# Keys and queries of four tiles loaded first, and one written order of four engines up to the first feed-forward matmul

## The chip, the cores and the metric

The kernel runs on one core of a Trainium2 chip. The metric is the device time of one execution in microseconds, here the median of three runs. A core has TensorE (PE, matmuls; its weight loads are shown apart as PEld), VectorE (DVE), ScalarE (ACT), GpSimd (POOL) and a queue engine, SyncE (SP), which here issues nearly all loads. Each of them works through its own list of instructions in order.

## The reference

Attention by chunks, then two feed-forward layers. q, k, v have 4 x 8 heads, 768 positions and 64 dimensions. Each chunk of 32 queries sees 8 memory keys and the keys from 16 before to 8 after it:

```python
for c in range(nc):
    k_full = np.concatenate([mem_k, k_ctx], axis=2)
    v_full = np.concatenate([mem_v, v_ctx], axis=2)
    scores = scale * np.matmul(q_c, k_full.transpose(0, 1, 3, 2))
    scores = scores - np.max(scores, axis=-1, keepdims=True)
    a = np.exp(scores)
    a = a / (np.sum(a, axis=-1, keepdims=True) + 1e-09)
    out[:, :, c_start:c_end] = np.matmul(a, v_full)
```

With the result laid out as x of 3072 tokens by 512, layer 1 is `h = x @ w_in; g = h - tanh(h); x = g @ w_out`, with a hidden width of 2048, and layer 2 the same with `g = max(h, 0) + alpha * min(h, 0)`.

## The kernel before

The tokens are 24 tiles of 128. A block is four tiles (512 tokens), so layer 1 has six blocks of 16 f-steps, one for each 128 of the hidden width. An f-step is a product h of 12 matmuls (`emit_h`, L274), the function g (`emit_g`, L289 to L299) and a product y of 12 (`emit_y`, L313). Every operand is kept as a high and a low half, and three of the four products of halves are made (`PASS`). The first matmul of h needs only the high halves; the second needs the low half of x, the third the low half of the weight.

Before the first h of block 0 the four tiles of its tokens go through attention. For a tile t: `emit_scores` makes the scores on PE (L590) into two PSUM banks, takes the maximum on DVE (L610, or L614 from tile 3 on), subtracts it (on POOL at L611 for tiles 0 to 2, with a copy of the scores by ACT at L609; on DVE at L615 after that) and takes the exponent on ACT (L619). `emit_soft` sums on DVE (L625 to L627), multiplies by the reciprocal on POOL (L628), and turns the result: for tiles 0 to 3 by matmuls with an identity on PE (`emit_turn`, L654 and L661, two halves hh) and a copy by ACT into the one buffer `ebuf` (L666); later by a DVE transpose and eight small copies (L635 to L644). `emit_pv` multiplies by the values (L674) and writes the token tile into the ring as high half by ACT (L681) and low half by DVE (L682).

Layer 1's weights arrive as raw 64-bit words. `split_w` makes two halves of each of an f-step's two weight tiles: a scaled copy by ACT (L105), three bit operations on DVE (L108, L111, L115; `to_f32`), then the high half by ACT (L121) and the low half by POOL (L122). `more_w` does that for one f-step and starts the loads of the step `AHEAD` later. In the opening loop it is called after tiles 1, 4 and 5 (`EARLY_W`), and in block 0 once for each f-step.

PSUM has eight banks: four in `ps_y` (turned tiles, early weight words, later y), two in `ps_h` (value products, h) and two in `ps_a` (scores, later weight words). Instructions are put in order by a planner that works with simulated times and the order of the code; within `tc.manual_schedule` the named engines keep the written order, and `tc.issue_after(i)` puts what is issued in it behind i on i's engine. Before, only SP's first loads are written by hand. While block 0 runs, a plan says after which half f-step the operations of tiles 4 and later come.

Of the kernel before, what the change touches and what calls it, by code (L numbers as in the profile page):

```python
# [7 lines left out]
FP32 = mybir.dt.float32  # L8
# [11 lines left out]
PERIOD = 20  # L20
LP, SLACK, LAST_C = 3, 2, 5
SPACE = 6
FIRST = 1
EARLY_W = (1, 4, 5)
PE_T = 4
ANCHOR = 'exp'
SUB_POOL = 3
ACT_COPIES = 4
BLOCKS1 = [4] * 6
# [2 lines left out]
AHEAD = 5  # L32
# [5 lines left out]
def chunk_attention_two_ffn_kernel(  # L38
# [51 lines left out]
    def load_raw(l, i, name):  # L90
        f, side = divmod(i, 2)
        src_i, src_o = (w_in1, w_out1) if l == 0 else (w_in2, w_out2)
        if l == 1 and f % 2:
            raw = ac.tile([128, 512], U64, tag="pk", name=name)
        else:
            raw = w_p.tile([128, 512], U64, tag="w", name=name)
        last["load"] = nc.sync.dma_start(out=raw, in_=src_o[f * 128:(f + 1) * 128, :] if side else src_i[f]).ins
        raws[l, i] = raw

    def to_f32(raw, dst=None):  # L100
        words = raw.bitcast(U32).rearrange("p (n two) -> p n two", two=2)
        lw, hw = words[:, :, 0], words[:, :, 1]
        pool, tag = (ps_y, "y") if stage.get("early") else (ps_a, "a")
        u = pool.tile([128, 512], U32, tag=tag, name="u")
        nc.scalar.activation(  # L105
            out=u.bitcast(FP32), in_=hw.bitcast(FP32), func=ACTF.Copy, scale=2.0 ** -112
        )
        nc.vector.tensor_scalar(  # L108
            out=u, in0=u, scalar1=3, scalar2=None, op0=ALU.logical_shift_left
        )  # L110
# [7 lines left out]
        return s.bitcast(FP32)  # L118

    def split_f32(v, hi, lo):  # L120
        nc.scalar.activation(out=hi, in_=v, func=ACTF.Copy)  # L121
# [456 lines left out]
    def half(x, j):  # L578
        return x.rearrange("q (p j) n -> q p j n", j=2)[:, :, j]

    def emit_scores(t):
        s = t % TPS
        kn = kt.pop(t)
        sps = [ps_a.tile([128, HP, 64], FP32, tag="a", name="sp",
                         padded_shape=[128, 8, 64]) for _ in range(2)]
        for p in range(HP):
            for c in range(4):
                for j in range(2):
                    r = slice(64 * j, 64 * j + 64)
                    last["at"] = nc.tensor.matmul(  # L590
                        out=sps[j][CH * c:CH * c + CH, p, :],
                        lhsT=qt[t][r, p, CH * c:CH * c + CH],
                        rhs=kn[r, p, c // 2, CH * (c % 2):CH * (c % 2) + W + NM],
                        start=True, stop=True,
                    ).ins
        for sp in sps:
# [4 lines left out]
        if t <= NS:  # L601
# [4 lines left out]
        mb = mx.to_broadcast([128, H, 64])  # L606
        if t < SUB_POOL:
            for j, sp in enumerate(sps):
                nc.scalar.activation(out=half(sc, j), in_=sp, func=ACTF.Copy)  # L609
                nc.vector.tensor_reduce(out=half(mx, j), in_=sp, op=ALU.max, axis=AX.X)  # L610
            nc.gpsimd.tensor_tensor(out=sc, in0=sc, in1=mb, op=ALU.subtract)  # L611
        else:
            for j, sp in enumerate(sps):
                nc.vector.tensor_reduce(out=half(mx, j), in_=sp, op=ALU.max, axis=AX.X)  # L614
# [5 lines left out]
        sm[t] = sc  # L620

    def emit_soft(t):
        sc = sm.pop(t)
        sg = aw.tile([128, H, 1], FP32, tag="sg", name="sg")
        nc.vector.tensor_reduce(out=sg, in_=sc, op=ALU.add, axis=AX.X)  # L625
        nc.vector.tensor_scalar(out=sg, in0=sg, scalar1=1e-9, scalar2=None, op0=ALU.add)
        nc.vector.reciprocal(out=sg, in_=sg)  # L627
        nc.gpsimd.tensor_tensor(  # L628
            out=sc, in0=sc, in1=sg.to_broadcast([128, H, 64]), op=ALU.mult
        )  # L630
        if t < PE_T:
            return emit_turn(sc)
        et = t_p.tile([128, 512], FP32, tag="t", name="et")
        et = et.rearrange("q (h s n) -> q h s n", h=H, s=2)
        nc.vector.transpose(out=et, in_=sc.rearrange("q h (s n) -> q h s n", s=2))  # L635
        for i in range(8):
            c, a = divmod(i, 2)
            r = CH * (c % 2 + a)
            o = ebuf[r:r + CH, c // 2, :, CH * (c % 2):CH * (c % 2) + CH]
            src = et[CH * c:CH * c + CH, :, a, :]  # L640
            if i < ACT_COPIES:
# [4 lines left out]
    def emit_turn(sc):  # L646
        idn = ident.rearrange("p (a c n) -> p a c n", a=2, c=2)
        for hh in range(2):
            tp = ps_y.tile([128, 512], FP32, tag="y", name="tp")
            tp = tp[:KW].rearrange("k (a h n) -> k a h n", a=2, h=4)  # L650
            for c in range(2):
                cols = slice(CH * c, CH * c + CH)
                r = 2 * CH * (1 - c)
                nc.tensor.matmul(  # L654
                    out=tp[r:r + CH, :, :, cols], lhsT=zeros, rhs=sc[:, 4 * hh:4 * hh + 4, :],
                    start=True, stop=True,
                )
                for h in range(4):
                    for a in range(2):
                        r = CH * (c + a)  # L660
                        nc.tensor.matmul(  # L661
                            out=tp[r:r + CH, :, h, cols],
                            lhsT=sc[:, 4 * hh + h, CH * a:CH * a + CH], rhs=idn[:, :, c, :],
                            start=True, stop=True,
                        )
            nc.scalar.activation(out=ebuf[:, :, 4 * hh:4 * hh + 4, :], in_=tp, func=ACTF.Copy)  # L666

    def emit_pv(t, slot):
        pv = ps_h.tile([128, 512], FP32, tag="h", name="pv")
        for p in range(HP):  # L670
            for a in range(2):
                for j in range(2):
# [1 line left out]
                    last["at"] = nc.tensor.matmul(  # L674
                        out=pv[D * j:D * j + D, 128 * p + 64 * a:128 * p + 64 * a + 64],
                        lhsT=vt[t][:, a, D * h:D * h + D],
                        rhs=ebuf[:, a, h, :],
                        start=True, stop=True,
                    ).ins
        pvv = pv.rearrange("k (p n) -> k p n", p=HP)  # L680
        nc.scalar.activation(out=ring[0][:, slot], in_=pvv, func=ACTF.Copy)  # L681
        nc.vector.tensor_tensor(  # L682
            out=ring[1][:, slot], in0=pvv, in1=f32(ring[0][:, slot]), op=ALU.subtract
        )

    first_of = {}
    t0 = 0
# [43 lines left out]
    if True:  # L731
# [19 lines left out]
            out=ident, in_=ident, compare_op=ALU.not_equal, fill=1.0, base=0,  # L751
            pattern=[[-1, 128]], channel_multiplier=1,
        )
        with tc.manual_schedule(engines={mybir.EngineType.SP}):
            loads_to(1)
            loads(1)
            loads_to(n0 - 1)
            load_v(n0 - 1)
            loads(2)
            loads_to(n0)  # L760
            load_v(NS)
        stage["early"] = True
        for t in range(n0 + 2):
            if t >= 2:
                tok_c(t - 2)
            if t <= n0:
                emit_scores(t)
            if t == n0:
                loads_to(n0 + 1)
            if 1 <= t:  # L770
                emit_soft(t - 1)
            for _ in range(EARLY_W.count(t)):
                more_w()
        stage["early"] = False
        plan = {}
        base, dur = [0], []
# [19 lines left out]
        pos = -4  # L796
        for t in range(n0 + 1, NTILE + 1):
            if t == n0 + 1:
                pos = 2
            else:  # L800
                lo = max(pos + SPACE, release(t - 1))
                pos = max(lo, int(at[t]) - SLACK)
# [171 lines left out]
```

## Time and profile before

| what | us |
|---|---|
| median of three runs | 1094.02 (1093.49 to 1094.47) |
| the profiled execution | 1096.97 |
| its span | 1094.1 |
| PE busy within it | 1056.4 |
| first matmul of the first h | 47.79 |
| dense run of h from | 50.37 |

The profile shows one execution. The time of an execution holds a little more than its span from the first to the last instruction, here 2.87 us. Times in the views are counted from the start of the span. A matmul of plain float32 operands (scores, turns, values) is recorded as two. Busy times can overlap within an engine, since one operation starts before the last has ended, and the recorded ends of matmuls are modelled.

### The profile page before, as it was taken

The page shows a single profiled execution, that of the slowest core. Times are in us where ns is not written, and L with a number is a line of the kernel's source. Part 1 is how long each engine was busy: PE and PEld are TensorE (multiplying, and loading weights), DVE is VectorE, ACT ScalarE, POOL GpSimd, SP SyncE. Part 2 cuts the span into 40 slices and gives each one's busy share as a digit, 9 for nine tenths or more (in the row PEclk, how much of TensorE's full clock was granted, in tenths as well). Part 3 has the DMA queues.
Part 4 walks back from the last instruction along what each step waited for, and adds up shares of the span by engine and source line. Part 5 has one row for each costly group of instructions (what it writes and reads, how often), then busy time and mean ns, then how long its engine had stood idle before and what let it go on. Part 6 is the DMA issues. An engine that isn't in the chain of part 4 may idle for free. (4 is left out here: it accounts for less than half of the span.)

```text
span 1094.1 us, 18216 instructions
## 1 busy us (share of the span) xinstructions
PE 1056.4 (97%) x6912; PEld 863.4 (79%) x6912; DVE 677.7 (62%) x1087; ACT 535.2 (49%) x956; POOL 464.3 (42%) x351
## 2 busy tenths in 40 slices
PE   4599999999999999999999999999999899999998
PEld 4478878888888888888888888878888688888786
DVE  3688855665776566576321255799555898456873
ACT  3466644444445444454342355655356564465650
POOL 3166634444454453445382122528222467124440
PEclk9699999999999999999999999999999999999999
DMA  9773143554555464454711355488844588833576
GB/s 269 276 259 127 59 145 123 203 168 168 179 184 181 156 204 164 174 174 150 221 32 36 145 176 199 131 265 271 259 170 148 181 248 277 244 135 138 153 213 170
DMA packets 99366, 196.22 MB, mean 179 GB/s; under 512 B 36560, under 2 KB 50896, under 8 KB 99280
## 3 DMA queue, kind: packets, MB, share of 16 engines
q1 hardware_dynamic: 93712, 188.52, 52.6%
q10 hardware_dynamic: 5568, 6.56, 1.7%
q8 instruction: 54, 0.88, 0.3%
q14 instruction: 32, 0.26, 0.1%
HBM read 153.10 MB, written 41.94 MB: 178 GB/s over the span
## 5 line engine op out<-in xcount | busy, mean ns | idle before, releaser
L274 PE MATMUL h<-ring,wt 128*128 128x512 f32 x1152 | 282.6, 393 | 5.9 <-ACT ring L681 2.4
L274 PEld LDWEIGHTS h<-ring,wt 128*128 128x128 f32 x1152 | 217.2, 189 | 52.7 <-ACT ring L681 2.6
L502 PE MATMUL yb<-go,wo 128*128 128x512 f32 x1008 | 235.5, 392 | 5.8 <-DVE go L483 2.7
L502 PEld LDWEIGHTS yb<-go,wo 128*128 128x128 f32 x1008 | 187.9, 188 | 51.1 <-DVE go L483 5.3
L408 PE MATMUL h<-xh,wi 128*128 128x512 f32 x672 | 212.1, 391 | 0.7 <-DVE gx L418 0.4
L299 POOL TENSOR_TENSOR gl<-t,gh 128x512 fp32r<-128x512 f32 x96 | 127.0, 1325 | 173.3 <-ACT gh L298 150.6
L313 PE MATMUL y<-gh,wt 128*128 128x512 f32 x768 | 192.8, 392 | 0.0
L313 PEld LDWEIGHTS y<-gh,wt 128*128 128x128 f32 x768 | 143.2, 188 | 30.4
L290 DVE TENSOR_TENSOR t<-h,t 128x512 f32<-128x512 f32 x96 | 65.9, 687 | 140.8 <-ACT t L289 140.6
L408 PEld LDWEIGHTS h<-xh,wi 128*128 128x128 f32 x672 | 126.2, 188 | 30.6 <-ACT hv L450 2.9
L289 ACT ACTIVATE t<-h 128x512 f32<-128x512 f32 x96 | 56.8, 592 | 112.2 <-PE h L274 92.8
L459 POOL TENSOR_TENSOR t<-gx,gy 128x512 f32<-128x512 f32 x24 | 31.1, 1295 | 175.1 <-DVE gy L418 175.1
L313 PE MATMUL y<-gl,wt 128*128 128x512 f32 x384 | 104.3, 390 | 0.0
L298 ACT ACTIVATE gh<-t 128x512 fp32r<-128x512 f32 x96 | 60.4, 629 | 54.2 <-DVE t L290 47.7
L313 PEld LDWEIGHTS y<-gl,wt 128*128 128x128 f32 x384 | 72.0, 188 | 15.0
L408 PE MATMUL h<-xl,wi 128*128 128x512 f32 x192 | 74.8, 390 | 0.0
L122 POOL TENSOR_TENSOR ws<-sm,ws 128x512 fp32r<-128x512 f32 x32 | 42.8, 1338 | 56.9 <-ACT ws L121 41.4
L417 ACT ACTIVATE n<-n,alpha_neg 128x512 f32<-128x512 f32 x96 | 65.9, 719 | 0.6
L122 POOL TENSOR_TENSOR wt<-s,wt 128x512 fp32r<-128x512 f32 x32 | 41.3, 1294 | 41.0 <-ACT wt L121 39.3
L483 DVE TENSOR_TENSOR go<-gx,go 128x512 fp32r<-128x512 f32 x42 | 57.3, 1406 | 1.4 <-ACT go L481 1.4
L408 PE MATMUL h<-x,wi 128*128 128x512 f32 x144 | 56.1, 390 | 0.0
L483 POOL TENSOR_TENSOR go<-gx,go 128x512 fp32r<-128x512 f32 x30 | 44.0, 1479 | 20.0 <-ACT go L481 20.0
(95 smaller groups left out, 1364.5 us busy)
## 6 DMA issues: line engine op xcount, KB each, us to landing
wo<-w2o SPq DMA_DIRECT2D x84, 512.0 KB, 4.2
wi<-w2i SPq DMA_DIRECT2D x72, 512.0 KB, 4.9
kn<-in_k_dram SPq DMA_DIRECT2D x24, 384.0 KB, 4.5
vn<-in_v_dram SPq DMA_DIRECT2D x24, 384.0 KB, 3.8
ri<-in_moe_w_in_dram SPq DMA_DIRECT2D x16, 512.0 KB, 7.7
ro<-in_moe_w_out_dram SPq DMA_DIRECT2D x16, 512.0 KB, 8.5
pk<-in_moe_w_in_dram SPq DMA_DIRECT2D x16, 512.0 KB, 4.0
pk<-in_moe_w_out_dram SPq DMA_DIRECT2D x16, 512.0 KB, 4.1
```

The costliest lines, as they stand in the source:

```text
L122: nc.gpsimd.tensor_tensor(out=lo, in0=v, in1=f32(hi), op=ALU.subtract)
L274: last["ffn"] = nc.tensor.matmul(out=h, lhsT=wi[:, a, kk, :], rhs=ring[c][:, s0:s0 + n, kk, :], start=(i == 0), stop=(i == 3 * KD - 1),).ins
L289: nc.scalar.activation(out=t, in_=h, func=ACTF.Tanh)
L290: last["dve"] = nc.vector.tensor_tensor(out=t, in0=h, in1=t, op=ALU.subtract).ins
L298: nc.scalar.activation(out=gh, in_=t, func=ACTF.Copy)
L299: nc.gpsimd.tensor_tensor(out=gl, in0=t, in1=f32(gh), op=ALU.subtract)
L313: mm = nc.tensor.matmul(out=yp[l, b][j][:, :n * 128], lhsT=wo[:, a, j * 128:(j + 1) * 128], rhs=g[c], start=first, stop=final,)
L408: nc.tensor.matmul(out=h, lhsT=w[:, a, 128 * kt:128 * kt + 128], rhs=x[c][:, kt, :], start=(first and j == 0), stop=(j == 5), skip_group_c ...
L417: nc.scalar.activation(out=n, in_=n, func=ACTF.Copy, scale=alpha_neg[:, f:f + 1])
L459: nc.gpsimd.tensor_tensor(out=d3, in0=gb[1], in1=ga[1], op=ALU.subtract)
L483: eng.tensor_tensor(out=op[:, 1], in0=src, in1=f32(op[:, 0]), op=ALU.subtract)
L502: nc.tensor.matmul(out=yd[b, into][i], lhsT=w[:, a, i], rhs=op[:, c], start=(m == into and p == 0 and n == 0), stop=(p == P2 - 1 and n == ...
```

## The change

- SP's list is written anew: k and q of tiles 0 to 3 first, then v of tiles 0 and 1, the raw w_in tile of step 0, v of tiles 2 and 3, the raw w_out tile of step 0, and only then step 1 and tile 4. A load of layer 2's weights is tied behind the last load issued.
- The helpers are cut into parts (scores_mm, scores_max, scores_sub, scores_exp, soft_sum, soft_mul, turn_mm, turn_copy, values_mm, values_hi, values_lo, scale_word, merge_words), and one list gives the order of these parts on PE, ACT, DVE and POOL up to the tokens of tile 3.
- Scores of tiles 1 and 3 use the banks of `ps_h`; the exponents of tiles 0 to 3 use four buffers of `g_p` (tags gh and gl); tiles 0 to 2 get their own turned buffer `eb` instead of `ebuf`.
- In a turn, the upper and lower half of an even chunk go in one matmul (28 matmuls a tile instead of 36).
- Only step 0's weights are split in the list; step 1's come behind the last low and high half of the tokens. Tile 4's scores and softmax move from before the first h to the first positions of the plan, and tile 5's from position 2 to 6.
- For tiles 4 to 7 all eight small copies are made by ACT, not four by ACT and four by DVE.

```diff
-FIRST = 1
-EARLY_W = (1, 4, 5)
-PE_T = 4
...
+            if l == 1:
+                after.enter_context(tc.issue_after(last["load"]))
+            last["load"] = nc.sync.dma_start(out=raw, in_=src).ins
...
+        pool, tag = (ps_h, "h") if t < NS and t % 2 else (ps_a, "a")
+        sps = [pool.tile([128, HP, 64], FP32, tag=tag, name="sp",
...
+        if t < NS:
+            sc = g_p.tile([128, H, 64], FP32, tag="gl" if t % 2 else "gh", name="sc")
...
+        copies = ACT_COPIES if t >= 2 * NS else 8
...
+                for a, m in ((0, 2),) if c == 0 else ((0, 1), (1, 1)):
+                    r = CH * (c + a)
+                    nc.tensor.matmul(
+                        out=tp[r:r + m * CH, :, h, cols],
+                        lhsT=sc[:, 4 * hh + h, CH * a:CH * (a + m)], rhs=idn[:, :, c, :],
...
+            eb[t] = ebuf if t == NS - 1 else w_p.tile([KW, 2, H, 2 * CH], FP32, tag="w", name="eb")
...
-        with tc.manual_schedule(engines={mybir.EngineType.SP}):
-            loads_to(1)
-            loads(1)
-            loads_to(n0 - 1)
-            load_v(n0 - 1)
+        with tc.manual_schedule(engines={E.SP}):
+            for t in range(n0):
+                load_k(t)
+                load_q(t)
+            load_v(0)
+            load_v(1)
+            load_raw(0, 0, "ri")
+            load_v(2)
+            load_v(3)
+            load_raw(0, 1, "ro")
             loads(2)
             loads_to(n0)
             load_v(NS)
...
-        for t in range(n0 + 2):
-            if t >= 2:
-                tok_c(t - 2)
-            if t <= n0:
-                emit_scores(t)
-            if t == n0:
-                loads_to(n0 + 1)
-            if 1 <= t:
-                emit_soft(t - 1)
-            for _ in range(EARLY_W.count(t)):
-                more_w()
...
+        with tc.manual_schedule(engines={E.PE, E.Activation, E.DVE, E.Pool}):
+            for fn, t in (
+                (scores_mm, 0), (scores_max, 0), (scores_sub, 0), (scores_exp, 0), (soft_sum, 0),
+                (scores_mm, 1), (soft_mul, 0), (scores_max, 1), (scores_sub, 1),
+                (scores_mm, 2), (turn, 0), (scores_max, 2), (scores_exp, 1), (soft_sum, 1),
+                (scores_sub, 2), (soft_mul, 1), (turned, 0), (scores_exp, 2), (soft_sum, 2),
+                (soft_mul, 2), (scores_mm, 3), (values_mm, 0), (scores_max, 3), (hi, 0), (lo, 0),
+                (scores_exp, 3), (soft_sum, 3), (soft_mul, 3), (turn, 1), (w_scale, 0),
+                (turned, 1), (w_merge, 0), (turn, 2), (w_split, 0), (values_mm, 1), (turned, 2),
+                (hi, 1), (lo, 1), (turn, 3), (values_mm, 2), (hi, 2), (turned, 3), (lo, 2),
+                (w_scale, 1), (values_mm, 3), (hi, 3), (lo, 3), (w_merge, 1), (w_split, 1),
+            ):
+                fn(t)
+        keep(0, 0, [half_w.pop(("w", i)) for i in range(2)])
+        nw[0] = 1
+        loads(AHEAD)
+        with tc.issue_after(last["hi"]), tc.issue_after(last["lo"]):
+            more_w()
...
-                pos = 2
+                assert release(n0) == 0
+                pos = 6
...
-                todo.append((release(n0), 10 * t - 9, tok_c, n0))
-                todo.append((a, 10 * t, emit_scores, t))
+                todo.append((0, 10 * n0, emit_scores, n0))
+                todo.append((1, 10 * n0 + 3, emit_soft, n0))
+                todo.append((1, 10 * n0 + 4, loads_to, t))
+                todo.append((a, 10 * t, both, t))
```

Here `scores_mm` of tile 3 takes the two banks of `ps_h` again, so `values_mm` of tile 0, which takes one of them next, stands behind the reading of tile 3's first half of scores.

## Rows read from the trace of the kernel before

**Rows 1.** The page: span, and busy time of each engine (share) and instructions.
```profile
span 1094.1 us, 18216 instructions
...
PE 1056.4 (97%) x6912; PEld 863.4 (79%) x6912; DVE 677.7 (62%) x1087; ACT 535.2 (49%) x956; POOL 464.3 (42%) x351
```

**Rows 2.** Table by stages: length, busy time (instructions), granted clock, DMA share, GB/s.
```profile
0.00:50.37 50.37, 25.50 (x737) 21.34 (x737) 23.80 (x55) 19.86 (x36) 13.48 (x19) 0.88 0.90 283
...
41.00:50.37 9.37, 2.50 (x38) 1.57 (x33) 9.37 (x19) 5.73 (x10) 2.98 (x3) 0.70 0.93 322
...
50.00:52.00 2.00, 1.63 (x4) 1.34 (x5) 1.91 (x4) 0.25 (x1) 0.97 (x1) 0.50 0.91 371
...
50.37:140.00 89.63, 89.63 (x702) 73.05 (x702) 73.09 (x140) 56.26 (x105) 58.44 (x47) 0.97 0.41 143
```

**Rows 3.** Timeline, 41 to 51 us: start, duration, engine, line, operation, [idle before, releaser].
```profile
41.13 1.89 DVE L108 TENSOR_SCALAR u<-u 128x512 uint32<-128x512 uint32 x3
...
44.41 0.93 PE L674 MATMUL pv<-ebuf,vn 96*64 96x64 f32 x16 [0.52 <-ACT ebuf L666]
...
46.62 0.63 ACT L121 ACTIVATE wt<-s 128x512 fp32r<-128x512 f32 x1 [1.57 <-DVE s L115]
...
47.16 0.58 ACT L681 ACTIVATE ring<-pv 128x512 fp32r<-128x512 f32 x1
...
47.79 0.79 PE L274 MATMUL h<-ring,wt 128*128 128x512 f32 x1 [2.45 <-ACT ring L681]
...
49.68 0.64 DVE L682 TENSOR_TENSOR ring<-pv,ring 128x512 fp32r<-128x512 f32 x1
...
50.37 7.64 PE L274 MATMUL h<-ring,wt 128*128 128x512 f32 x23 [1.79 <-DVE ring L682]
```

**Rows 4.** Groups by line on DVE, 41 to 50.5 us: busy, mean ns.
```profile
L108 DVE TENSOR_SCALAR u<-u 128x512 uint32<-128x512 uint32 x6 | 4.0, 690 | 0.0
```

**Rows 5.** Timeline of SP's queue: issue of q of tiles 2 and 3.
```profile
4.66 0.69 SPq L567 DMA_DIRECT2D qn<-in_q_dram  x1
...
8.38 0.33 SPq L567 DMA_DIRECT2D qn<-in_q_dram  x1
```

**Rows 6.** Issues within 4.6 to 5.3 and 8.3 to 9 us: KB, us to landing.
```profile
qn<-in_q_dram SPq DMA_DIRECT2D x1, 256.0 KB, 10.4
...
qn<-in_q_dram SPq DMA_DIRECT2D x1, 256.0 KB, 11.4
```

**Rows 7.** Timeline, tile 1's scores on PE.
```profile
8.50 1.53 PE L590 MATMUL sp<-kn,qn 64*32 64x64 f32 x64 [2.59 <-DMA qn<-in_q_dram]
```

**Rows 8.** Groups of one turn's matmuls, 0 to 20 and 38.9 to 41.3 us.
```profile
L654 PE MATMUL tp<-sc,marks 128*32 128x256 f32 x8 | 3.6, 634 | 0.0
...
L654 PE MATMUL tp<-sc,marks 128*32 128x256 f32 x8 | 2.0, 383 | 0.0
```

**Rows 9.** Groups by line and shape, 0 to 64 us: busy, mean ns, idle before.
```profile
L122 POOL TENSOR_TENSOR wt<-s,wt 128x512 fp32r<-128x512 f32 x10 | 12.7, 1287 | 21.1 <-ACT wt L121 21.1
...
L666 ACT ACTIVATE ebuf<-tp 96x512 f32<-96x512 f32 x8 | 4.7, 586 | 9.4 <-PE tp L661 9.4
...
L625 DVE TENSOR_REDUCE sg<-sc 128x8 f32<-128x512 f32 x5 | 3.4, 684 | 7.4 <-ACT sc L619 7.4
...
L619 ACT ACTIVATE sc<-sc 128x512 f32<-128x512 f32 x5 | 3.1, 626 | 8.4 <-POOL sc L611 6.3 <-DVE sc L615 2.1
...
L615 DVE TENSOR_TENSOR sc<-sp,mx 128x256 f32<-128x256 f32 x4 | 1.5, 415 | 0.0
```

**Rows 10.** Timeline, a value product and scores in block 0.
```profile
98.90 1.15 PE L674 MATMUL pv<-ebuf,vn 96*64 96x64 f32 x32
...
99.98 0.86 PE L590 MATMUL sp<-kn,qn 64*32 64x64 f32 x64
```

**Rows 11.** Timeline, one product h in block 0.
```profile
82.49 2.88 PE L274 MATMUL h<-ring,wt 128*128 128x512 f32 x12
```

**Rows 12.** Timeline of DVE in block 0, before tile 5's scores.
```profile
65.82 0.09 DVE L600 MEMSET sp<- 32x32 f32 x1 [3.77 <-PE sp L590]
```

More of the change, by code (lines that the diff above doesn't have):

```diff
@@ L22 @@
 SPACE = 6
-FIRST = 1
-EARLY_W = (1, 4, 5)
-PE_T = 4
-ANCHOR = 'exp'
 SUB_POOL = 3
@@ L96, in load_raw, with words_of, scale_word @@
             raw = w_p.tile([128, 512], U64, tag="w", name=name)
-        last["load"] = nc.sync.dma_start(out=raw, in_=src_o[f * 128:(f + 1) * 128, :] if side else src_i[f]).ins
+        src = src_o[f * 128:(f + 1) * 128, :] if side else src_i[f]
+        with ExitStack() as after:
+            if l == 1:
+                after.enter_context(tc.issue_after(last["load"]))
+            last["load"] = nc.sync.dma_start(out=raw, in_=src).ins
         raws[l, i] = raw
-    def to_f32(raw, dst=None):
+    def words_of(raw):
         words = raw.bitcast(U32).rearrange("p (n two) -> p n two", two=2)
-        lw, hw = words[:, :, 0], words[:, :, 1]
+        return words[:, :, 0], words[:, :, 1]
+    def scale_word(raw):
         pool, tag = (ps_y, "y") if stage.get("early") else (ps_a, "a")
@@ L105, in to_f32, with merge_words @@
         nc.scalar.activation(
-            out=u.bitcast(FP32), in_=hw.bitcast(FP32), func=ACTF.Copy, scale=2.0 ** -112
+            out=u.bitcast(FP32), in_=words_of(raw)[1].bitcast(FP32), func=ACTF.Copy, scale=2.0 ** -112
         )
+        return u
+    def merge_words(raw, u, dst=None):
+        lw, hw = words_of(raw)
         nc.vector.tensor_scalar(
@@ L118, in to_f32 @@
         return s.bitcast(FP32)
+    def to_f32(raw, dst=None):
+        return merge_words(raw, scale_word(raw), dst)
     def split_f32(v, hi, lo):
@@ L579, in half, with scores_mm @@
         return x.rearrange("q (p j) n -> q p j n", j=2)[:, :, j]
-    def emit_scores(t):
-        s = t % TPS
+    def scores_mm(t):
         kn = kt.pop(t)
-        sps = [ps_a.tile([128, HP, 64], FP32, tag="a", name="sp",
+        pool, tag = (ps_h, "h") if t < NS and t % 2 else (ps_a, "a")
+        sps = [pool.tile([128, HP, 64], FP32, tag=tag, name="sp",
                          padded_shape=[128, 8, 64]) for _ in range(2)]
@@ L595, in emit_scores, with scores_max @@
                     ).ins
+        spt[t] = sps
+    def scores_max(t):
+        s = t % TPS
+        sps = spt.pop(t)
         for sp in sps:
@@ L600, in emit_scores @@
                 nc.vector.memset(sp[128 - CH:128, :, 64 - R_CTX:64], NEG)
-        if t <= NS:
+        if t < NS:
+            sc = g_p.tile([128, H, 64], FP32, tag="gl" if t % 2 else "gh", name="sc")
+        elif t == NS:
             sc = g_p.tile([128, H, 64], FP32, tag="gh", name="sc")
@@ L605, in emit_scores @@
         mx = aw.tile([128, H, 1], FP32, tag="mx", name="mx")
-        mb = mx.to_broadcast([128, H, 64])
-        if t < SUB_POOL:
-            for j, sp in enumerate(sps):
+        for j, sp in enumerate(sps):
+            if t < SUB_POOL:
                 nc.scalar.activation(out=half(sc, j), in_=sp, func=ACTF.Copy)
[L610 to L614, printed above, removed]
+            nc.vector.tensor_reduce(out=half(mx, j), in_=sp, op=ALU.max, axis=AX.X)
+            if t >= SUB_POOL:
                 nc.vector.tensor_tensor(
@@ L618, in emit_scores, with scores_sub, scores_exp, soft_sum @@
                 )
-        last["exp"] = nc.scalar.activation(out=sc, in_=sc, func=ACTF.Exp, scale=scale).ins
-        sm[t] = sc
-    def emit_soft(t):
-        sc = sm.pop(t)
+        sm[t] = sc, mx
+    def scores_sub(t):
+        sc, mx = sm[t]
+        nc.gpsimd.tensor_tensor(
+            out=sc, in0=sc, in1=mx.to_broadcast([128, H, 64]), op=ALU.subtract
+        )
+    def scores_exp(t):
+        sc = sm[t] = sm[t][0]
+        last["exp"] = nc.scalar.activation(out=sc, in_=sc, func=ACTF.Exp, scale=scale).ins
+    def emit_scores(t):
+        scores_mm(t)
+        scores_max(t)
+        scores_exp(t)
+    def soft_sum(t):
         sg = aw.tile([128, H, 1], FP32, tag="sg", name="sg")
-        nc.vector.tensor_reduce(out=sg, in_=sc, op=ALU.add, axis=AX.X)
+        nc.vector.tensor_reduce(out=sg, in_=sm[t], op=ALU.add, axis=AX.X)
         nc.vector.tensor_scalar(out=sg, in0=sg, scalar1=1e-9, scalar2=None, op0=ALU.add)
         nc.vector.reciprocal(out=sg, in_=sg)
+        sgt[t] = sg
+    def soft_mul(t):
+        sc, sg = sm[t], sgt.pop(t)
         nc.gpsimd.tensor_tensor(
@@ L630, in emit_soft @@
         )
-        if t < PE_T:
-            return emit_turn(sc)
+    def emit_soft(t):
+        soft_sum(t)
+        soft_mul(t)
+        sc = sm.pop(t)
         et = t_p.tile([128, 512], FP32, tag="t", name="et")
@@ L640, in emit_soft @@
             src = et[CH * c:CH * c + CH, :, a, :]
-            if i < ACT_COPIES:
+            if i < copies:
                 nc.scalar.activation(out=o, in_=src, func=ACTF.Copy)
@@ L644, in emit_soft, with turn_mm @@
                 nc.vector.tensor_copy(out=o, in_=src)
-    def emit_turn(sc):
+    def turn_mm(t, hh):
+        sc = sm[t]
         idn = ident.rearrange("p (a c n) -> p a c n", a=2, c=2)
[L648 to L666, printed above, removed]
@@ L668, in emit_pv @@
-    def emit_pv(t, slot):
+        tp = ps_y.tile([128, 512], FP32, tag="y", name="tp")
+        tp = tp[:KW].rearrange("k (a h n) -> k a h n", a=2, h=4)
+        for c in range(2):
+            cols = slice(CH * c, CH * c + CH)
+            r = 2 * CH * (1 - c)
+            nc.tensor.matmul(
+                out=tp[r:r + CH, :, :, cols], lhsT=zeros, rhs=sc[:, 4 * hh:4 * hh + 4, :],
+                start=True, stop=True,
+            )
+            for h in range(4):
+                for a, m in ((0, 2),) if c == 0 else ((0, 1), (1, 1)):
+                    r = CH * (c + a)
+                    nc.tensor.matmul(
+                        out=tp[r:r + m * CH, :, h, cols],
+                        lhsT=sc[:, 4 * hh + h, CH * a:CH * (a + m)], rhs=idn[:, :, c, :],
+                        start=True, stop=True,
+                    )
@@ L669, in emit_pv, with turn_copy, values_mm @@
+        tpt[t, hh] = tp
+    def turn_copy(t, hh):
+        if hh == 0:
+            eb[t] = ebuf if t == NS - 1 else w_p.tile([KW, 2, H, 2 * CH], FP32, tag="w", name="eb")
+        nc.scalar.activation(
+            out=eb[t][:, :, 4 * hh:4 * hh + 4, :], in_=tpt.pop((t, hh)), func=ACTF.Copy)
+    def values_mm(t):
+        e = eb.pop(t, ebuf)
         pv = ps_h.tile([128, 512], FP32, tag="h", name="pv")
@@ L676, in emit_pv, with values_hi, values_lo @@
                         lhsT=vt[t][:, a, D * h:D * h + D],
-                        rhs=ebuf[:, a, h, :],
+                        rhs=e[:, a, h, :],
                         start=True, stop=True,
                     ).ins
[L680 to L684, printed above, removed]
+        pvt[t] = pv.rearrange("k (p n) -> k p n", p=HP)
+    def values_hi(t, slot):
+        last["hi"] = nc.scalar.activation(out=ring[0][:, slot], in_=pvt[t], func=ACTF.Copy).ins
+    def values_lo(t, slot):
+        last["lo"] = nc.vector.tensor_tensor(
+            out=ring[1][:, slot], in0=pvt.pop(t), in1=f32(ring[0][:, slot]), op=ALU.subtract
+        ).ins
+    def emit_pv(t, slot):
+        values_mm(t)
+        values_hi(t, slot)
+        values_lo(t, slot)
+    spt, sgt, tpt, eb, pvt = {}, {}, {}, {}, {}
     first_of = {}
@@ L753, in chunk_attention_two_ffn_kernel @@
         )
-        with tc.manual_schedule(engines={mybir.EngineType.SP}):
-            loads_to(1)
-            loads(1)
-            loads_to(n0 - 1)
-            load_v(n0 - 1)
+        E = mybir.EngineType
+        with tc.manual_schedule(engines={E.SP}):
[8 more added lines that the diff above has]
+            load_raw(0, 1, "ro")
+            nl[0], nk[0] = 1, n0
             loads(2)
@@ L762, in chunk_attention_two_ffn_kernel, with w_scale, w_merge, w_split @@
         stage["early"] = True
-        for t in range(n0 + 2):
-            if t >= 2:
-                tok_c(t - 2)
-            if t <= n0:
-                emit_scores(t)
-            if t == n0:
-                loads_to(n0 + 1)
-            if 1 <= t:
-                emit_soft(t - 1)
-            for _ in range(EARLY_W.count(t)):
-                more_w()
+        half_w = {}
+        def w_scale(i):
+            half_w[i] = raws.pop((0, i))
+            half_w[i] = half_w[i], scale_word(half_w[i])
+        def w_merge(i):
+            half_w[i] = merge_words(*half_w[i])
+        def w_split(i):
+            w = w_p.tile([128, 2, 512], FP32R, tag="w", name="wt")
+            split_f32(half_w.pop(i), w[:, 0], w[:, 1])
+            half_w["w", i] = w
+        def turn(t):
+            turn_mm(t, 0)
+            turn_mm(t, 1)
+        def turned(t):
+            turn_copy(t, 0)
+            turn_copy(t, 1)
+        def hi(t):
+            values_hi(t, x0[0][0] + t)
+        def lo(t):
+            values_lo(t, x0[0][0] + t)
+        with tc.manual_schedule(engines={E.PE, E.Activation, E.DVE, E.Pool}):
[16 more added lines that the diff above has]
+            more_w()
         stage["early"] = False
```

## The prediction

> **What bounds the kernel now.** I read the page first: TensorE (PE) is busy for 1056.4 of 1094.1 us [rows 1], so 38 us are all that better feeding could return. The table by stages says where they lie: up to 50.37 us PE works 25.5 us, and from there to 140 us it has no gap at all [rows 2]. So the question is only when the first product h starts, and whether PE can then run on without a gap. The timeline just before that point shows what h waits for [rows 3]: the value products of tile 3 (pv) end at about 45.3, ScalarE (ACT) copies them (ring, high half) only at 47.16, because a weight copy stood ahead of it in ACT's order and that one waited for VectorE (DVE); DVE writes the low half at 49.68, and the dense run of h begins at 50.37. The stage table for 41 to 50.37 shows why: DVE is busy for all of 9.37 us [rows 2], and the grouped rows of DVE there show what with: six shifts of weight words, each one of the three operations that a weight tile costs [rows 4]. DVE is preparing weights of later steps while h waits for two short operations of tile 3.
>
> **Where the first h lands after the change.** I walk the written order, engine by engine, with durations from rows.
>
> Loads. q of tile 2 was issued at 4.66 and landed 10.4 us later, at 15.1; q of tile 3 at 8.38 plus 11.4, at 19.8 [rows 5, 6]. In these 4.7 us came one v, one k and one q, 1024 KB, so a k and q (640 KB) take 2.9 us. The new list on SP's queue puts k and q of tiles 2 and 3 in front of v and the weights. PE began tile 1's scores at 8.50, when its q was there [rows 7], and nothing ahead of that moves. So q of tile 2 comes at about 11.5, of tile 3 at 14.5; the first v (1.8 us each) at 16.2, and w_in, after a second v, at 20.4 at that rate: later than before, but ahead of their uses below (19.1 and 21.5). The load of layer 2's weight that used to slip into this queue is tied behind the last load: 512 KB less in the way. What stands behind all this on SP (k and v of tile 4, raw weights) has its uses later than 32 us.
>
> Chain. From tile 2's q at 11.5:
> - scores 2: 1.5 us, as tile 1's [rows 7]; turn 0: a turn took 3.6 us early and 2.0 us later [rows 8]; by the code it had 36 matmuls and now has 28, so 2.8 or 1.55. I take 2.8 here, as this is as early. Ends 15.8.
> - then, in ACT's order, the second turn copy 0.59 and exp 2 0.63; on DVE the sum of tile 2, 0.68 plus two tiny operations, 1.13 [rows 9]. Ends 18.2.
> - pv of tile 0 needs a bank that tile 3's first half of scores leaves: that is a new wait of PE on DVE, for a reduce and a subtract of half a tile, 0.8 us together. Turn 1 and turn 2 are queued behind it. pv then takes 1.15 us [rows 10]. Ends 20.2.
> - copy of pv 0.59, exp 3 0.63, sum 3 1.13: 22.7. Weight merge on DVE: three operations of 0.69 us, of which three in a row took 1.89 [rows 3, 4]; 1.85. Its copy on ACT 0.63: 25.2. The copies of turn 2 stand behind this one on ACT, another new wait.
> - two copies 1.16, pv 2 1.15, its copy 0.59, two copies of turn 3 1.16, pv 3 1.15, its copy 0.59, low half 0.66 on DVE.
> These are 19.8 us, and 18 hand-overs of 0.05 us (47.16 plus 0.58 to 47.79 is one [rows 3]) make 20.5: **the dense run of h starts at 32.0 us**. Bounds: with PE at its faster pace from the start the same walk gives 30.5; with the slow pace throughout (2.8 for each turn, and each pv longer in the ratio 3.6 to 2.0, 2.1) it gives 39.2. I keep 32.0, which has the slow pace up to 17.4 and the faster one after that: before, too, the turns went from the one pace to the other after some us of close work, and the new order has PE working closely from 11.5.
>
> **What comes after it.** One f-step is 24 matmuls. Twelve of them span 2.88 us, with 0.39 for one, so they start 0.227 us apart and a step is 5.44 us [rows 11]. DVE needs 6 weight operations and one subtract for a step, 4.3 us at the spacing of those three: it keeps up, but catches up by only 1.1 us a step. Before, 23 matmuls from 50.37 took 7.64 us instead of 5.21 [rows 3], at a granted clock of 0.50 at first, the lower level [rows 2]; one matmul had run already, so the effective start was 52.6.
> After: (a) the second h needs w_in of step 1, and DVE has w_out of step 0 ahead of it: two merges 3.7, copy 0.63, GpSimd subtract 1.3 [rows 9], so the low half is there 5.6 us after the start, when h wants it (third matmul) at 3.2. PE loses 2.4 us. If the clock is low instead, h itself takes those 2.4 us and the wait vanishes, so this is counted once. (b) Work that DVE did before the first h now comes after it: step 1's and most of step 2's weights, tile 4's maximum, subtract and sum, about 8.6 us, against 1.1 of slack a step. Most is wanted only some steps later; I take 2 us, between nothing and 7.5, which is two waits like the 3.8 us that DVE once sat behind a scores product in its order [rows 12]. (c) tile 4's scores are now PE work after the start: 0.86 [rows 10].
> Effective start 32.0 + 2.4 + 2.0 + 0.9 = 37.3, against 52.6: **15.3 us earlier**. Everything later goes by steps and carries over. The profiled execution took 1096.97 with a span of 1094.1; its span would become 1078.8. The runs' median is 1094.02, so I forecast 1079.
>
> **Costed at nothing.** Four more small copies for each of tiles 4 to 7 go from DVE to ACT: 16 operations, each of fewer elements than a turn copy, so under 9.4 us in all. ACT is busy for 56.3 of the 89.6 us from 50.37 to 140 [rows 2] and hides them; without that room up to 9.4 us would be lost, less what DVE wins. The three turned buffers take weight slots until about 30 us, when raw weights of steps 2 to 4 still find room. Splitting functions and merged turn matmuls: in the walk.
>
> **The rule on the clock.** PE's matmuls of one shape take 634 ns on average before 20 us and 383 around 40 us [rows 8], and the clock was at the lower level at 50 us, after a stretch with 2.5 us of PE work in 9.37 [rows 2]. The Trainium skill, "TensorE: Matmul & The Clock Gate", section "HAM oscillation", says that waits between bursts can put the engine back to half rate for each burst. By rows I charge 2.4 us once; by that rule each step of the first block that begins with a wait could be charged again.
>
> **Rivals.**
> 1. *The first block starves.* In-order DVE waits for tile 4's and 5's scores while the next weights queue behind: (b) is 7.5 instead of 2. For it: no lead of prepared weights, where the old code prepared those of three steps in its opening loop. Against it: no PE gap in 50 to 140 though DVE was as full. Gain 9.8, or 7.4 if also the walk gives 34.4 (PE fast only from 25 us on): 1084 to 1087. Chance 0.20.
> 2. *PE stays slow through the whole head.* Start 39.2, effective 44.5: gain 8.1, 1086. For it: many short bursts with waits. Against: by the walk PE works for some 10 of the 12 us from 19 on. Chance 0.08.
> 3. *The other side: slower.* Waits for weights put the clock back again and again, and the steps of the first block run at half rate: 5.44 us lost in each. From the third such step on (15.3 / 5.44 = 2.8) the gain is gone; five make 1106. For it: the lead is nothing. Against: a step at half rate takes 10.9 us, in which DVE prepares more than two steps of weights, so PE then works without a gap, and work without a gap brought the pace back before: only 2.4 us were lost in 23 matmuls [rows 3]. Chance 0.07.
> 4. *It does not do what it says.* The late loads or ACT's strict order hold the first h near 48. Loads would have to be 25 us later than walked. 1092 to 1096. Chance 0.05.
> 5. The forecast, 1075 to 1083: 0.60.
>
> **Numbers.** 0.2% (2.2 us) is about what a measurement of this kernel can tell from no change. Faster: cases 1, 2 and 5, 0.88; same: 0.05; slower: 0.07. The best sum (30.5, no further stalls) is 33.8, a gain of 18.8, 1075; the worst (39.2 and 7.5) 50.0, a gain of 2.6, 1091. The range leaves out the worst of case 1 with 2, and cases 3 and 4: 1074 to 1088.
>
> **What would show it.** First h dense between 30 and 34 us, low half of tile 3 just before it; k and q of tile 3 landed by 15; DVE with gaps before 32 us, full after; PE waiting some 2.4 us before the second h, on GpSimd's or ACT's weight split, or a clock at the lower level there. It is wrong if ACT's copies of turns wait longer for the weight merge than walked, if PE idles over 5 us in the 40 us after the first h, or if the clock is at its lower level for over 10 us there.

## The result and the profile after

The changed kernel takes 1106.57 us (median of four runs, 1104.93 to 1107.25) against 1093.76 before (four runs by now); the ratio is 1.0111, interval 1.0098 to 1.0124. It is slower by 12.8 us where 15 us less were forecast. The profiled executions differ by 10.6 us (spans 1104.7 and 1094.1); the one of before was 3 us above its own median, so the two profiles show a little less than the medians do.

The dense run of h does start earlier, at 42.34 instead of 50.37 [rows 3]. The stores of layer 1's first block tell what became of that. These are the lines of those stores, before and in the changed kernel (duration, first and last start):

```profile
L339 ACTq DMA_DIRECT2D y1d<-ys x24: 326/456/1492, 154.0 to 632.3; - x24
...
L348 ACTq DMA_DIRECT2D y1d<-ys x24: 326/431/1780, 163.1 to 642.6; - x24
```

So 8.0 us are gained at the start of block 0 and 9.1 us are lost at its end: 17.1 us more in between. The rest of the kernel adds 1.5 more in these profiles. The table by stages (columns as in rows 2) gives block 0 before in its first row. The others are of the changed kernel: a piece of the head at the lower clock, the head's last part, block 0 as a whole, and three pieces of it:

```profile
50.37:154.00 103.63, 103.63 (x791) 84.63 (x792) 83.30 (x162) 63.90 (x120) 63.12 (x52) 0.98 0.40 142
...
22.59:28.50 5.91, 5.91 (x63) 4.05 (x64) 3.63 (x9) 2.24 (x4) 1.22 (x2) 0.50 1.04 329
...
29.00:39.20 10.20, 9.56 (x199) 7.19 (x196) 0.69 (x2) 3.48 (x7) 1.27 (x1) 1.00 1.02 385
...
42.33:163.10 120.77, 109.51 (x854) 86.52 (x855) 90.76 (x169) 75.10 (x145) 67.24 (x55) 0.94 0.39 136
...
44.00:46.00 2.00, 2.00 (x6) 1.52 (x6) 2.00 (x5) 0.00 (x0) 0.00 (x0) 0.54 0.00 0
...
66.00:68.00 2.00, 0.00 (x0) 0.00 (x0) 0.62 (x2) 1.94 (x6) 0.00 (x0) 0.58 1.03 420
...
70.00:72.00 2.00, 1.85 (x5) 1.36 (x5) 1.97 (x4) 1.08 (x2) 2.00 (x3) 0.50 0.00 0
```

PE idles for 120.77 - 109.51 = 11.3 us in a stage that had no idle time before, and after each of the longer waits the granted clock is at its lower level (0.50 is 1.2 GHz), so that busy time grows too. The row from 29.00 us is the other half of the story: for ten microseconds shortly before the first h, DVE works 0.69 us, although the raw w_out of step 0, issued at 10.88, landed 13.0 us later, and the raw w_in of step 1, issued at 12.87, after 12.2. The view of waits of PE from 40 to 200 us (sum, count, longest):

```profile
PE h L283 <- ACT wt L130: 6.8, 3, 6.0
PE y L322 <- ACT gh L307: 2.3, 1, 2.3
PE h L283 <- POOL wt L131: 1.9, 3, 0.6
PE h L283 <- DVE t L299: 1.6, 1, 1.6
```

The last of these falls after block 0, and the kernel before has it too (1.6 us). The 6.0 us wait is the fourth h's. The timeline around it:

```profile
56.33 0.99 PE L599 MATMUL sp<-kn,qn 64*32 64x64 f32 x64
...
58.90 0.63 ACT L107 ACTIVATE u<-ri 128x512 f32<-128x512 f32 x1 [0.41 <-DVE sc L627]
...
64.77 0.65 DVE L121 SCALAR_TENSOR_TENSOR s<-ri,u 128x512 uint32<-128x512 uint32 x1
64.88 3.40 ACT L675 ACTIVATE ebuf<-et 32x256 f32<-32x256 f32 x8 [3.76 <-DVE et L667]
...
68.30 0.63 ACT L130 ACTIVATE wt<-s 128x512 fp32r<-128x512 f32 x1
...
68.98 5.22 PE L283 MATMUL h<-ring,wt 128*128 128x512 f32 x12 [5.99 <-ACT wt L130]
```

Read it from the bottom: h waits for the high half of the fourth step's w_in (ACT, 68.30). DVE had that word ready at 65.42, but ACT first makes the eight small copies of tile 4, 3.40 us. And the whole preparation of that weight began only at 58.90, behind tile 4's scores (56.33) in the order. The twelve matmuls then take 5.22 us, at the lower clock; such a product takes 2.88 [rows 11].

### The profile page after: what moved, and what is told of

It reads as the page before. It is cut to its first block, busy times and chain, and to the rows that moved or that the text cites. A ratio compares the mean times of both kernels' runs of the same rounds, so it can differ in the third digit from the quotient of the medians.

```text
span 1104.7 us, 18081 instructions
## 1 busy us (share of the span) xinstructions
PE 1064.4 (96%) x6848; PEld 863.9 (78%) x6848; DVE 671.7 (61%) x1071; ACT 540.8 (49%) x972; POOL 462.8 (42%) x351
## 5 line engine op out<-in xcount | busy, mean ns | idle before, releaser
L114 DVE TENSOR_SCALAR u<-u 128x512 uint32<-128x512 uint32 x64 | 44.2, 695 | 21.8 <-ACT u L107 21.8
```

The costliest lines, as they stand in the source:

```text
L114: nc.vector.tensor_scalar(out=u, in0=u, scalar1=3, scalar2=None, op0=ALU.logical_shift_left)
```

## The experiments

Block 0's end is the first store of layer 1's result in each profile. Each ratio is to runs of the kernel before beside it, whose medians lie between 1093.8 and 1094.9 us.

| run | median, us | ratio to before | dense h | end of block 0 |
|---|---|---|---|---|
| kernel before | 1093.76 | 1 | 50.37 | 154.0 |
| changed kernel | 1106.57 | 1.0111 (1.0098 to 1.0124) | 42.34 | 163.1 |
| e1_narrow | 1106.60 | 1.0111 (1.0094 to 1.0128) | 44.85 | 166.1 |
| e2_copies | 1097.87 | 1.0033 (1.0018 to 1.0047) | 41.52 | 156.5 |
| e3_tile4 | 1104.92 | 1.0094 (1.0075 to 1.0113) | 44.81 | 160.4 |
| e4_lead | 1103.80 | 1.0086 (1.0067 to 1.0105) | 41.21 | 159.7 |
| c1_copies_later | 1096.04 | 1.0011 (0.9998 to 1.0025) | 41.55 | 154.8 |
| c2_copies_lead | 1097.80 | 1.0031 (1.0019 to 1.0043) | 40.97 | 155.1 |
| c3_copies_lead_later | 1096.68 | 1.0016 (1.0007 to 1.0025) | 40.74 | 153.5 |
| c4_old_copies | 1096.48 | 1.0019 (1.0008 to 1.0029) | 48.31 | 153.4 |
| d1_fill | 1091.36 | 0.9976 (0.9967 to 0.9986) | 44.11 | 151.9 |
| d2_fill_only | 1098.57 | 1.0039 (1.0026 to 1.0052) | 39.62 | 154.3 |
| c5_old_loads | 1095.00 | 1.0005 (0.9996 to 1.0014) | 49.92 | 153.2 |
| c6_old_wide | 1094.66 | 1.0001 (0.9992 to 1.0011) | 45.48 | 149.5 |

**The form of the turn (e1, c6).**

```diff
-                for a, m in ((0, 2),) if c == 0 else ((0, 1), (1, 1)):
+                for a, m in ((0, 1), (1, 1)):
```

> The changed kernel with the 36 narrow turn matmuls of before. Theory A, the head is late because a turn with the 64-wide matmuls takes longer: turns 2 and 3 go from 3.3 us to about 2.0 each, the first two shrink too, and the dense run of h starts at 37 to 39 us instead of 42.3; as everything after it hangs on that start, the time falls to 1101 to 1104 us. Rival, the turns were slow from the clock alone: start and time unchanged, 1105 to 1107.

The turn did get shorter, and the start did not move forward. The timeline of PE in e1_narrow:

```profile
12.74 0.63 PE L687 MATMUL tp<-sc,marks 128*32 128x256 f32 x1
12.75 0.31 PE L694 MATMUL tp<-marks,sc 128*32 128x64 f32 x1
16.39 0.74 PE L694 MATMUL tp<-marks,sc 128*32 128x64 f32 x11 [3.01 <-issue]
...
28.56 0.38 PE L687 MATMUL tp<-sc,marks 128*32 128x256 f32 x1
28.57 0.39 PE L694 MATMUL tp<-marks,sc 128*32 128x64 f32 x7
...
29.44 0.38 PE L687 MATMUL tp<-sc,marks 128*32 128x256 f32 x1
...
32.38 0.50 PE L694 MATMUL tp<-marks,sc 128*32 128x64 f32 x11 [2.34 <-issue]
```

Half a turn now takes 0.88 us (28.56 to 29.44), but PE stops in the middle of turns for 3.0, 2.3 and 2.2 us, and for 1.2 us in a value product, released by nothing that the profile shows ("issue"). For the changed kernel, half of turn 2 on PE's timeline:

```profile
29.65 0.59 PE L687 MATMUL tp<-sc,marks 128*32 128x256 f32 x2
30.17 0.68 PE L694 MATMUL tp<-marks,sc 128*64 128x64 f32 x8
30.78 0.40 PE L687 MATMUL tp<-sc,marks 128*32 128x256 f32 x1
30.79 0.42 PE L694 MATMUL tp<-marks,sc 128*32 128x64 f32 x8
...
31.27 0.59 PE L687 MATMUL tp<-sc,marks 128*32 128x256 f32 x2
```

That is 1.62 us from 29.65 to 31.27, at the faster pace: fewer matmuls, more time. The lines show where it goes: 32-wide matmuls run beside the zeroing matmul of 256 columns (28.56 and 28.57, 30.78 and 30.79), the 64-wide ones from 30.17 run with none beside them. The wide form costs 0.7 us for each half of a turn, but PE loses 8.7 us in four stops in e1_narrow and 1.84 in one in the changed kernel. Theory A is right on the length of a turn and wrong on the start and the time.

In c6 the kernel before gets the wide form alone:

```diff
-                    for a in range(2):
+                    for a, m in ((0, 2),) if c == 0 else ((0, 1), (1, 1)):
```

> The kernel before with the 64-wide turn matmuls alone (28 a tile instead of 36). If the wide form costs what the changed kernel showed, a turn at the faster pace takes 3.2 us instead of 2.0; if PE stops after the same counts of instructions, its stops come later in the work. The old head has slack on PE, so 1093 to 1097 us.

No change in time. In its profile PE has no stop in the head, where before had two of 5.5 us together, h is dense at 45.48 and block 0 ends at 149.5, each over 4 us earlier than before:

```profile
45.48 7.03 PE L274 MATMUL h<-ring,wt 128*128 128x512 f32 x23 [2.59 <-DVE ring L682]
```

The time did not follow. What comes after block 0 takes 943.3 us in this profile and 940.1 before; over the fourteen profiles it runs from 939.3 to 943.3. So the end of block 0 in one profile gives a kernel's time to some 4 us only, and the medians decide.

**The eight copies (e2, c4).**

```diff
-        copies = ACT_COPIES if t >= 2 * NS else 8
+        copies = ACT_COPIES
```

> The changed kernel with tiles 4 to 7 copied by four ACT and four DVE operations again. Theory B, the eight copies stand ahead of a weight copy on ACT: the 6.0 us wait before the fourth h falls to about 4.3 and the waits of 0.4 to 0.6 us near tiles 5 to 7 go away; 1102 to 1104 us. Rival, DVE is the bound there and gets 1.2 us more for each tile: 1106 to 1109.

The gain is 8.7 us, about twice the upper end of the expectation; 6.6 of it stand at the end of block 0. PE's waits from 20 to 250 us in e2_copies:

```profile
PE h L283 <- ACT wt L130: 4.3, 1, 4.3
PE y L322 <- ACT gh L307: 2.5, 1, 2.5
```

The long wait fell by 1.7 us, as expected from 3.40 us of copies that became 1.70. The shorter waits for weight halves of ACT and POOL near tiles 5 to 7 went too, as expected: they were 2.7 us together. With a start that is 0.8 us earlier that makes 5.2 of the 6.6 us; some 1.5 us less busy time is the rest, and the expectation had no term for it. c4 makes the reverse edit in the kernel before:

```diff
-            if i < ACT_COPIES:
+            if i < (ACT_COPIES if t >= 2 * NS else 8):
```

> The kernel before, with all eight copies of tiles 4 to 7 on ACT and nothing else changed. Theory B with a lead: before, weights are two steps ahead, so a weight copy that comes 1.7 us later on ACT is still in time: 1094 to 1096 us. Rival, the eight copies cost as such, 2 us for each of four tiles: 1099 to 1103.

It costs 0.19% (0.08 to 0.29%), about 2 us. The same copies cost 8.7 us in the changed kernel, and 6.0 with the weights of one more step ahead (e4 against c2, below). So the price of these operations on ACT is not set by ACT's free time alone; that it is set by how far the weights are ahead fits all three numbers but is not shown, since the kernels before and after differ in more than the lead.

**Tile 4 and the lead of weights (e3, e4, c1 to c3).** e3 puts tile 4 back before the first h:

```diff
             more_w()
+        emit_scores(n0)
+        loads_to(n0 + 1)
+        emit_soft(n0)
...
-                pos = 6
+                pos = 2
...
```

> The changed kernel with tile 4's scores and softmax issued before the first h again, and its tokens and tile 5's scores at the old positions. Theory C, tile 4's chain inside the first f-steps is what holds back the fourth step's weight: the 6.0 us wait goes, the first h comes at most 2 us later; 1097 to 1101 us. Rival D, only the lead of prepared weights is missing: the waits come back under other names, 1104 to 1108.

1104.92: a gain of 2 us instead of 6 to 10, not clear of noise, as rival D had it. The planner put tile 4's scores into the head, where PE waited 7.5 us for that tile's q; the first h came 2.5 us later, and the waits came back shared between ACT's and POOL's weight halves. e4 calls `more_w` twice ahead of the first h:

```diff
-            more_w()
+            for _ in range(2):
+                more_w()
```

> The changed kernel with the weights of three steps instead of two issued before the first h. Rival D, the lead is what is missing: the wait before the fourth h falls by the time of one step's weights, 1101 to 1104 us. Theory C, tile 4's chain is ordered ahead of the next weights whatever the lead: one step later the same wait, 1105 to 1108.

1103.80, 3 us gained; a wait of 4.7 us for a weight half stayed, beside new ones of 2.7 us for a weight half of the second step and, behind block 0, of 2.6 us for g. Neither theory alone. The next three start from four and four copies; c1 moves tile 4 to positions 4 and 5 and tile 5 to 10, c2 has the extra `more_w`, c3 both.

```diff
-                pos = 6
+                pos = 10
...
-                todo.append((0, 10 * n0, emit_scores, n0))
-                todo.append((1, 10 * n0 + 3, emit_soft, n0))
-                todo.append((1, 10 * n0 + 4, loads_to, t))
+                todo.append((4, 10 * n0, emit_scores, n0))
+                todo.append((5, 10 * n0 + 3, emit_soft, n0))
+                todo.append((5, 10 * n0 + 4, loads_to, t))
```

> The changed kernel with four and four copies, and tile 4's scores at position 4 and softmax at 5 of block 0 instead of 0 and 1 (tile 5's at 10 instead of 6). Theory C, tile 4's chain ahead of the fourth step's weight makes the 4.3 us wait that was left with four and four copies (1097.9 us): the wait goes or shrinks below 2 us, 1092 to 1095 us. Rival D, the lead is missing and DVE has the same sum of work: the wait only moves to a later h, 1096 to 1099.

> The changed kernel with four and four copies and the weights of three steps issued ahead of the first h. Rival D, the lead is missing: 1092 to 1095 us. Theory C, tile 4's chain stands in the order ahead of the next weight whatever the lead: gain over four and four alone like the 2.8 us that the lead gave to the changed kernel, with a wait of 3 us or more at a later h, 1094 to 1098.

> Both at once: four and four copies, three steps' weights ahead, tile 4 at positions 4 and 5. If both C and D hold a part: no PE wait over 2 us after the first h but the one before the first y, and 1088 to 1092 us, faster than the kernel before. If the head's gain of 8 us is eaten by the clock and by the first y alone: 1093 to 1096.

1096.04, 1097.80 and 1096.68: moving tile 4 gains 1.8 us more, which the intervals do not tell from nothing, and the weights of an extra step behind the first h's inputs gain nothing. In c1 the list of waits still shows the fourth step's kind of wait, now 2.6 us, and the 2.4 us before the first y. c3 misses both of its forecasts: its waits are others, 3.5 us for g's subtract on DVE among them. Shifting DVE's work within block 0 moves waits about; that its sum in the first steps stays the same is the likely reason, not measured.

**Weights into the gaps of the head (d1, d2).** The list is changed in its second half, so that the rest of step 0's weights and all of step 1's are prepared while PE turns tiles 2 and 3:

```diff
-                (turned, 1), (w_merge, 0), (turn, 2), (w_split, 0), (values_mm, 1), (turned, 2),
-                (hi, 1), (lo, 1), (turn, 3), (values_mm, 2), (hi, 2), (turned, 3), (lo, 2),
-                (w_scale, 1), (values_mm, 3), (hi, 3), (lo, 3), (w_merge, 1), (w_split, 1),
+                (turned, 1), (w_merge, 0), (w_scale, 1), (turn, 2), (w_split, 0), (values_mm, 1),
+                (turned, 2), (w_merge, 1), (hi, 1), (lo, 1), (turn, 3), (w_split, 1),
+                (w_scale, 2), (w_merge, 2), (w_scale, 3), (w_split, 2), (values_mm, 2), (hi, 2),
+                (turned, 3), (w_merge, 3), (lo, 2), (values_mm, 3), (hi, 3), (lo, 3), (w_split, 3),
...
```

d2 is the changed kernel with this alone; d1 also has c1's edits.

> The changed kernel with only these weights written into the gaps; eight copies on ScalarE and tile 4 at positions 0 and 1 stay. Theory E with a lead of one step: the wait before the first y goes and the 6.0 us wait before the fourth h falls by 2 to 4 us, 1097 to 1102 us. Rival, the eight copies and tile 4 hold the later steps whatever is prepared: 1103 to 1107.

> Four and four copies, tile 4 at positions 4 and 5, and the weights of the second half of step 0 and of step 1 written into the list, into the gaps that VectorE has from 29 to 39 us in the changed kernel. Theory E, the written order leaves VectorE idle while the weights wait, so the first steps starve and the clock falls with each wait: the first h stays at 40 to 42 us, the 2.4 us wait before the first y and the 2.6 us wait later go away, 1087 to 1092 us, faster than the kernel before. Rival, what the first steps lose comes from the clock after the sparse head whatever is ready: 1094 to 1097.

d2 gains 8 us with the copies and tile 4 where they were: the wait before the first y is gone, the long one is 4.7 us, a fall of 1.3 where 2 to 4 were expected. d1 takes 1091.36, 0.24% less than before (0.14 to 0.33%) and 4.7 us less than c1, from which only these weights set it apart: theory E holds for the time. Its profile is of its slowest execution, 1094.98 us. Its timeline and the stage table of its block 0:

```profile
44.11 9.87 PE L283 MATMUL h<-ring,wt 128*128 128x512 f32 x35 [0.23 <-DVE ring L726]
```

```profile
44.11:151.90 107.79, 104.67 (x849) 85.13 (x850) 89.56 (x172) 64.23 (x121) 64.44 (x53) 0.97 0.39 133
```

PE idles 3.1 us in block 0 instead of 11.3, and the first 35 matmuls of h run through, nearly three products with no wait between them. One wait is left there, 3.1 us for g's subtract on DVE. Theory E missed the start: 44.11 instead of 40 to 42, with a stop of PE of 2.4 us in that head; in d2, with the same list, h is dense from 39.62.

**The order of loads alone (c5).** The kernel before with the new list on SP's queue:

```diff
-            loads_to(1)
-            loads(1)
-            loads_to(n0 - 1)
-            load_v(n0 - 1)
+            for t in range(n0):
+                load_k(t)
+                load_q(t)
+            load_v(0)
+            load_v(1)
+            load_raw(0, 0, "ri")
+            load_v(2)
+            load_v(3)
+            load_raw(0, 1, "ro")
...
```

> The kernel before with the new order of loads on the queue alone. The head before was held by VectorE and ScalarE, which prepared weights, not by loads: dense run of h at 48 to 52 us, 1092 to 1097 us. Rival, loads held it: dense run at 42 to 46, 1087 to 1091.

No change; the dense run starts at 49.92. The old head was not held by loads. That the order on DVE and ACT held it is read from rows 2 to 4; no run changes that order alone, and c6's earlier head says that the form of the turns and PE's stops held a part of it.

## Why the prediction was wrong

What bounds the kernel was read rightly in the main: time is lost before the dense run of h and in PE's run behind it. c5 confirms that loads did not hold the old head. That DVE's and ACT's order was all that held it is not shown, as c6 says. The two terms of the sum both failed, by 10.3 and 14.0 us.

**The walk, 32.0.** The dense run came at 42.3. The step that failed is the turn: its length, taken as "2.8 or 1.55" by counting matmuls, and its place, since the walk lets turns 1 to 3 run beside the chain of ACT and DVE. Turn 0 ended at 19.2 instead of 15.8, with a stop of 1.84 us in it. The first value product then ended at 24.5 instead of 20.2: PE was at the lower clock again, and that clock held to about 28.5, 0.50 from 22.59, where the walk has the faster pace from 17.4 on. Turn 1 took 5.2 us, turns 2 and 3 took 3.3 us each at the faster pace. From 24.5 on PE itself was the bound, busy 9.56 of 10.20 us from 29.0, and ACT's copies waited for turns, not for the weight merge. That lost the other 6.0 us. The loads were forecast well: tile 2's scores began at 11.00 instead of 11.5. The walk also has a slip that matters little: its terms add up to 19.9 and its hand-overs to 0.9, so that it should have read 32.3.

**The price behind the start, 5.3.** On the forecast's scale it was 19.3: 17.1 more than before plus the 2.2 that before lost itself. Term (a), 2.4 us, came true in size, but as a wait of the first y (2.33), which the planner had put ahead of the second h: g's subtract stood behind the merges on DVE. Tile 4's scores, term (c), took 0.99. The step that failed is term (b), mis-sized, "I take 2 us, between nothing and 7.5": with the copies costed at nothing it came to 16.0. Some 9 of these are waits, nearly all for weight halves, and 7 are busy time at the lower clock: 4.9 more than before, whose own 2.2 come on top. The mechanism is the starved first block of rival 1. Of the two causes named there the runs price the missing lead of weights at 8.0 us (d2), and tile 4's place in the order at about 2 (e3, c1), not clear of noise.

**"Costed at nothing".** This is the step that cost most in one piece: the eight copies, hidden by ACT's idle share of 50 to 140 us. They cost 8.7 us, near the bound that the text gave for lost cover (under 9.4), though by another way: 1.7 us of it is the long wait, 2.7 the shorter ones, 1.5 busy time, and 0.8 an earlier start; the rest falls behind block 0. The share was an average; the copies stood in ACT's order in front of a weight half that PE was waiting for. The gains of e2 and d2 overlap: together with tile 4's move they make 15.2 us (d1), not 16.7.

**The rivals.** Rival 1 had the mechanism but gave it 7.5 us. Rival 2, PE slow through the whole head, came in part: the lower clock lasted to 28.5, and the start was later than the 39.2 it gave. Rival 3, the other side, had its time, 1106, with a clock that falls after waits: near 44 to 46, 50 to 52 and 70 to 72 us the granted clock was 0.54 and 0.50. The prediction's argument against it was half right: work without a gap did bring the clock back each time, but the next waits set it back again: 1.2 and 0.7 us around the last value product, 2.3 before the first y, 6.0 before the fourth h. The short waits of 0.4 to 0.6 us behind 90 us did not; the clock from there to 163 us was 1.00. For the clock the prediction charged 2.4 us once; the rows give 7.1, nearly three times that, for three stretches at the lower level. The trace agrees here with the rule of the Trainium skill ("TensorE: Matmul & The Clock Gate", section "HAM oscillation") that waits between bursts can put the engine back to half rate for each burst. The clock was not the larger part, though: idle time was, 11.3 us. Rival 4 did not come.

With the weights written into the gaps and the copies shared again, the same order of loads and turns gives the fastest kernel here, so the earlier start could be kept; how much of d1's 0.24% is the start's was not tried.

## What to carry to other kernels

When the first product is made earlier, look at what the next three products need and whether that is ready: here an earlier start with no lead was paid back, with a lower clock on top. A free share of an engine over a stage hides nothing that stands in its order ahead of what the bounding engine waits for; ask for each added operation what is queued behind it. And fill a written order until the engines that prepare the next stage have no long gaps in it.

## What the hardware showed beyond that

PE's stops with no releaser in the profile stand at the same counts of its own matmuls in all these kernels, while the load queue is full. In the changed kernel:

```profile
15.12 0.39 PE L687 MATMUL tp<-sc,marks 128*32 128x256 f32 x1
17.34 0.40 PE L687 MATMUL tp<-sc,marks 128*32 128x256 f32 x1 [1.84 <-issue]
```

Up to this stop the timeline holds 221 recorded matmuls, and e1_narrow stops first after 221 as well, though it is at another place in the turn; its next stops follow after 126, 128 and 127 more. The kernel before has two such stops, after 348 and 475, in its waits of PE up to 64 us:

```profile
PE tp L661 <- issue: 5.5, 2, 4.1
```

In the other profiles, too, every such stop before the first h stands after 221, 347 or 348, 475, or 601 or 602 matmuls. But not each of these places has a stop: the changed kernel has one only, and e3, c3 and c6 have none. The four kernels with narrow turns lose 4.3 to 8.7 us in them, the ten with wide turns 0 to 2.4.

Loads of instructions that come late because the queues are full of data could do this: the table of DMA queues for 14 to 15 us, just ahead of the stop in the changed kernel, lists one packet of the instruction queue:

```profile
q1 hardware_dynamic: 69, 0.24, 101.5%
q8 instruction: 1, 0.02, 7.8%
```

That cause is argued, not shown: c6 has such a packet between 20 and 22 us and no stop, and no run here thins the loads and keeps the instructions.

A matmul with a weight of 64 columns between ones of 32 is slow in a way that its count does not show: 1.62 us for a half turn with 14 matmuls against 0.88 with 18. The lines above show that the 64-wide ones have nothing running beside them; why was not tried.
